# Attention output by query rows and a later transpose, in place of an output that is transposed from the start

## The chip, the cores and the metric

The kernel runs on one core of a Trainium2 chip. The metric is the device time of one execution in microseconds (us); lower is better. The engines are TensorE (PE, with its weight loads shown apart as PEld), VectorE (DVE), ScalarE (ACT), GpSimd (POOL) and SyncE (SP). All of them run their own instructions in order and wait for each other by semaphores. Matrix products are written to PSUM, which has eight banks per partition here.

## What is computed

Two parts follow each other: an attention over sorted blocks, and an expert layer on its output. Cut to what matters:

```python
# attention: B=4, H=8, S=768, D=64, 8 blocks of 96 rows
P = sort_net                                   # (4, 8, 8, 8)
for _ in range(5):                             # rows and columns made to sum to one
    P = exp(P - P.max(-1)); P /= P.sum(-1); P /= P.sum(-2)
k_s = einsum('bhij,bhjcd->bhicd', P, k_blocks); v_s = the same with v
attn = softmax(q_block @ k_s.T / 8)            # 96 x 96 per block
x = attn @ v_s                                 # -> (3072, 512): 4*768 rows, 8*64 columns
# expert layer: 3072 rows, 512 columns, 8 experts, 1024 hidden
G = exp(x @ w_gate - max)
for _ in range(8):                             # Sinkhorn rounds
    G /= G.sum(1); G /= G.sum(0); G *= 3072 / 8
out = sum over e of G[:, e] * (relu(x @ w1[e]) @ w2[e])
```

## The kernel before

**Stages.** (1) 0 to 14.4 us: the sorting matrix is made by DVE and ACT while PE runs 36 products that nobody reads (L131). `Pbig` is copied out of PSUM (L157). (2) The attention, from 14.4 us. (3) Sinkhorn on the gates `glog` (L348 to L360). (4) The gates go to DRAM and back (L370, L389), and the expert layer runs in 24 units (from L672 on), seven products of a Strassen scheme each. PE's first product of unit 0 starts at 154.1 us.

**The attention loop (L295 to L315).** Sixteen pairs of heads go through three steps, and 19 iterations `m` run them staggered: `stage1(m)`, `stage2(m-1)`, `stage3(m-2)`.

- `stage1` (L173) sorts K and V with products against the expanded matrix `R` (L182), transposes Q (L193), and copies five PSUM banks to SBUF: three by ACT (L187), V's second and Q by DVE (L189, L196). It then builds the next pair's `R` on DVE (L167).
- `stage2` (L200) makes the scores of eight blocks (L208), has ACT take their exponential into `ATT` (L211), transposes V (L215) and lets DVE copy it to `VS` (L218). There the 96 rows of a block lie on partitions, and each of 8 blocks x 2 heads has 64 columns.
- `stage3` (L220) works in two halves of four blocks. A product with `ones64` (L226) puts the sums of the exponentials on 64 partitions for each head. ACT makes the reciprocal out of Ln and Exp (L229, L230). The products of L234 have `VS` as weights and `ATT` as the moving side, so that the output has head columns on partitions, 64 for each head of the pair. DVE multiplies by the reciprocal and writes `xtT` (L236), which is x transposed.

Between the steps stands `fill(1)`, four per iteration. It gives PE a block of the expert layer's first product (`h_block`, L259: four products of 512 columns, L264), as soon as the batches that it reads are done (`state["done"]`, L315); before that, it gives a product that nobody reads (`spin`, L277, L280). The blocks' relu goes to DVE (L268) and ACT (L270) in turn; there are 88 blocks in all. `gate(b)` (L240) makes the gate logits of a batch (L244) and their exponential (L246). Up to iteration 5 the fills are spins.

All PSUM tiles here come from one pool of eight banks (`bank`). A bank is given out again when its last reader is done.

**Sinkhorn.** Each of eight rounds runs on DVE: row sums (L349), reciprocal (L350), product (L351), column sums (L353). Three blocks go to PE (`fill(3)`), then the matmul that adds over partitions (L356), and DVE ends the round (L357, L358). Then `gbf` is copied (L363), one block follows (`fill(1)`), `gp` is transposed (L367), copied to `gTs` (L369) and sent out. Eight differences of weights (`w2_sums(0, ...)`, L346, two for each of four results) stand next, and at last the remaining 11 blocks.

**What sets the order.** Each part is recorded under a manual schedule, in which an engine's instructions keep the order of the source. Two parts that follow each other (the Sinkhorn part and the expert part) are recorded apart.

Of the kernel before, what the change touches and what calls it, by code (L numbers as in the profile page):

```python
# [13 lines left out]
F32 = mybir.dt.float32  # L14
BF16 = mybir.dt.bfloat16
F16 = mybir.dt.float16
AF = mybir.ActivationFunctionType
AX = mybir.AxisListType
ALU = mybir.AluOpType
ENG = mybir.EngineType  # L20

def mkap(t, dims, off=0):
    return bass.AP(tensor=t.tensor, offset=t.offset + off, ap=dims)

@with_exitstack
def kernel(
# [11 lines left out]
    nc = tc.nc  # L38
    B, H, S, D = 4, 8, 768, 64
    NB = 8  # L40
    NPAIR = 16
    N, Dm, E, F = 3072, 512, 8, 1024
    NT = 24
    KB = 1024
    scale = 1.0 / (D ** 0.5)

    ones = ctx.enter_context(tc.tile_pool(name="ones", bufs=1))
# [3 lines left out]
    def bank(shape, dt=F32):  # L51
        return ps.tile(shape, dt, name="bank")
# [3 lines left out]
    def carve(shape, dt, off):  # L56
        n = 1
        for d_ in shape[1:]:
            n *= d_
        n = n * (2 if dt == F32 else 1)  # L60
        v_ = bigf[:, off // 2:off // 2 + n]
        if dt == F32:
            v_ = v_.bitcast(F32)
        names = "abcd"[:len(shape) - 1]
        return v_.rearrange("p (" + " ".join(names) + ") -> p " + " ".join(names),
                            **{k_: d_ for k_, d_ in zip(names, shape[1:])})
# [3 lines left out]

    warm = ones.tile([128, 1], F32)
    nc.vector.memset(warm, 0.0)
    nc.scalar.preload_act_table_set("natural_log_exp_and_others")
    nc.scalar.activation(out=warm, in_=warm, func=AF.Exp)

    wide = carve([128, 512], BF16, 98 * KB)
# [1 line left out]
    ident = ones.tile([128, 128], BF16)  # L78
    make_identity(nc, ident)
    identh = ones.tile([128, 128], F16)  # L80
    nc.vector.tensor_copy(identh, ident)
    ones64 = ones.tile([128, 64], BF16)
    nc.vector.memset(ones64, 1.0)
    ones32 = ones.tile([128, 128], F32)
    nc.vector.memset(ones32, 1.0)
    mask = ones.tile([128, 16], F32)
# [7 lines left out]
    atp_ = actx.enter_context(tc.tile_pool(name="atp", bufs=2))  # L94
# [13 lines left out]
    w1t, w2t = {}, {}  # L108

    def load_w1(e):  # L110
        w1t[e] = w1r[W1S[e]]
        nc.gpsimd.dma_start(out=w1t[e], in_=moe_w1[e].rearrange("(kk k) f -> k kk f", k=128))
# [10 lines left out]
    xtT = ones.tile([128, 4, B, 6, 128], BF16)  # L123
# [14 lines left out]
    for it in range(5):  # L138
# [4 lines left out]
                                op=ALU.mult)  # L143
        nc.vector.reduce_sum(out=rs, in_=Pt, axis=AX.X)
        nc.vector.reciprocal(out=rs, in_=rs)
        if it < 4:
            nc.vector.tensor_tensor(out=Pt, in0=Pt, in1=mkap(rs, [rs.ap[0], rs.ap[1], [0, 8]]),
                                    op=ALU.mult)
        else:
            nc.vector.tensor_tensor(out=Prep, in0=mkap(P, [P.ap[0], [8, 8], [1, 8], [0, 16]]),  # L150
                                    in1=mkap(rs, [rs.ap[0], [0, 8], [1, 8], [0, 16]]), op=ALU.mult)
# [4 lines left out]
    Pbig = carve([128, 8, 32], F32, 90 * KB)  # L156
    nc.vector.tensor_copy(Pbig, pbp)  # L157

    KT, VT, QT, ATT, VS = {}, {}, {}, {}, {}

    vs_ = [carve([128, 8, 2, 64], BF16, (91 + 3 * n) * KB)[0:96] for n in range(2)]

    Rt = {}

# [35 lines left out]
    def stage2(m):  # L200
        ATT[m] = [atp_.tile([96, 2, 384], BF16, name=f"at{h2}") for h2 in range(2)]
        for half in range(2):
            bb = [bank([96, 4, 96]) for _ in range(2)]
            for i4 in range(4):
                i = half * 4 + i4
                for h2 in range(2):
                    hs = slice(64 * h2, 64 * h2 + 64)
                    nc.tensor.matmul(bb[h2][:, i4, :], KT[m][hs, i].rearrange("d kk c -> d (kk c)"),  # L208
                                     QT[m][hs, :, 16 * i:16 * i + 16], start=True, stop=True)
            for h2 in range(2):  # L210
                nc.scalar.activation(out=ATT[m][h2][:, half, :], in_=bb[h2].rearrange("k i q -> k (i q)"),  # L211
                                     func=AF.Exp, scale=scale)
        b_ = bank([96, 8, 128], BF16)
        for i in range(8):
            nc.tensor.matmul(b_[:, i, :], VT[m][:, i].rearrange("d kk c -> d (kk c)"), ident, is_transpose=True,  # L215
                             start=True, stop=True)
        VS[m] = vs_[m % 2]
        nc.vector.tensor_copy(VS[m], b_.rearrange("c i (h d) -> c i h d", d=64))  # L218

    def stage3(m):  # L220
        b, hpi = m // 4, m % 4
        xo = xtT[:, hpi, b].rearrange("d kk (i c) -> d i kk c", c=16)
        for half in range(2):
            den = bank([128, 384])
            for h2 in range(2):
                nc.tensor.matmul(den[64 * h2:64 * h2 + 64, :], ones64[0:96], ATT[m][h2][:, half, :],  # L226
                                 start=True, stop=True)
            rc = atp_.tile([128, 384], F32, name="rc")
            nc.scalar.activation(out=rc, in_=den, func=AF.Ln)  # L229
            nc.scalar.activation(out=rc, in_=rc, func=AF.Exp, scale=-1.0)  # L230
            b_ = bank([128, 4, 96])
            for i4 in range(4):
                for h2 in range(2):
                    nc.tensor.matmul(b_[64 * h2:64 * h2 + 64, i4, :], VS[m][:, half * 4 + i4, h2, :],  # L234
                                     ATT[m][h2][:, half, 96 * i4:96 * i4 + 96], start=True, stop=True)
            nc.vector.tensor_tensor(out=xo[:, 4 * half:4 * half + 4],  # L236
                                    in0=b_.rearrange("d i (kk c) -> d i kk c", c=16),
                                    in1=rc.rearrange("d (i kk c) -> d i kk c", i=4, c=16), op=ALU.mult)

    def gate(b):  # L240
        b_ = bank([128, 6, E])
        for t in range(6):
            for kk in range(4):
                nc.tensor.matmul(b_[:, t, :], xtT[:, kk, b, t, :], wg[:, kk], start=(kk == 0),  # L244
                                 stop=(kk == 3))
        nc.scalar.activation(out=glog[:, 6 * b:6 * b + 6, :], in_=b_, func=AF.Exp)  # L246
# [35 lines left out]
    def fill(n, both=True):  # L282
        for _ in range(n):
            if state["h"] >= len(blocks):
                return
            e, c, fb = blocks[state["h"]]
            if last_batch[c] > state["done"]:
                if state["done"] < 0:
                    spin(1)
                return  # L290
            h_block(e, c, fb, both)
            state["h"] += 1

    build_r(0)
    for m in range(NPAIR + 3):  # L295
        if m < NPAIR:
            stage1(m)
        if m + 4 < NPAIR:
            load_pair(m + 4)
        if m == 0:  # L300
            load_w1(0)
        if m == 5:
            load_w1(1)
        fill(1)
        if 1 <= m <= NPAIR:
            stage2(m - 1)
        fill(1)
        if 2 <= m <= NPAIR + 1:
            stage3(m - 2)
        fill(1)  # L310
        if m >= 6 and m % 4 == 2:
            gate(m // 4 - 1)
        fill(1)
        if m >= 5 and m % 4 == 1:
            state["done"] = m // 4 - 1  # L315

    order.__exit__(None, None, None)
# [5 lines left out]
    w2T = [r2.tile([128, 2, 4, 256], BF16, name=f"w2T{n}") for n in range(3)]  # L323
# [14 lines left out]
    rs2 = ones.tile([128, NT], F32)  # L338
    cs2 = ones.tile([128, E], F32)
    cs1 = ones.tile([128, E], F32)  # L340
    def w2_sums(p, k, i):
        w = w2t[2 * p + i]
        B11, B12, B21, B22 = (w[:, 4 * fh:4 * fh + 4, 256 * dh:256 * dh + 256] for fh in range(2) for dh in range(2))
        T1, T2, T4 = (t[:, i] for t in w2T)
        o_, a, b = ((T1, B12, B11), (B12, B22, B12), (T2, B22, T1), (T4, B21, T2))[k]
        nc.vector.tensor_tensor(out=o_, in0=a, in1=b, op=ALU.subtract)  # L346

    for it in range(8):  # L348
        nc.vector.reduce_sum(out=rs2, in_=glog, axis=AX.X)  # L349
        nc.vector.reciprocal(out=rs2, in_=rs2)  # L350
# [1 line left out]
                                op=ALU.mult)  # L352
        nc.vector.reduce_sum(out=cs2, in_=glog.rearrange("p t e -> p e t"), axis=AX.X)  # L353
        fill(3, both=False)
        b_ = bank([128, E])
# [3 lines left out]
                                       in1=mkap(cs1, [cs1.ap[0], [0, NT], cs1.ap[1]]),  # L359
# [1 line left out]
    gbf = ones.tile([128, E, NT], F16)  # L361
    gTs = carve([128, 2, 128], BF16, 108 * KB)[0:96].bitcast(F16)
    nc.vector.tensor_copy(gbf, glog.rearrange("p t e -> p e t"))  # L363
    fill(1, both=False)
    gp = bank([96, 2, 128], F16)
    for n in range(2):
        nc.tensor.matmul(gp[:, n, :], gbf.rearrange("p e t -> p (e t)")[:, 96 * n:96 * n + 96], identh,  # L367
                         is_transpose=True, start=True, stop=True)
    nc.vector.tensor_copy(gTs, gp)  # L369
    nc.sync.dma_start(out=gdr.rearrange("(n r) p -> r n p", n=2), in_=gTs)  # L370
    for k in range(4):
        for i in range(2):
            w2_sums(0, k, i)
    fill(len(blocks), both=False)
    order.__exit__(None, None, None)
    pctx.close()
# [23 lines left out]
    def w1_sums(e, part):  # L400
        w = w1t[e]
        A11, A12, A21, A22 = (w[:, 2 * kh:2 * kh + 2, 512 * fh:512 * fh + 512] for fh in range(2) for kh in range(2))
        S1, S2, S4 = wS[e % 2]
        o_, a, b, op = ((S1, A21, A22, ALU.add), (S2, S1, A11, ALU.subtract), (A21, A11, A21, ALU.subtract),
                        (S4, A12, S2, ALU.subtract))[part]
        nc.vector.tensor_tensor(out=o_, in0=a, in1=b, op=op)

    def relu_add(out, a, b):
        nc.vector._custom_dve(TENSOR_ADD_SAT, out=out, in0=a, in1=b, s0=3.4028234663852886e38, s1=0.0)  # L409
# [194 lines left out]
    for n in range(3, NU):  # L604
        nq = NDQ.get(n, 4)
        nd = min(nq, len(l1) - first_dq)
        for d_ in range(nd):
            for st in range(4):
                q = 28 * n + (28 * d_) // nq + (0, 3, 5, 9)[st] * (28 // nq) // 7
# [3 lines left out]
    for q in sorted(when):  # L613
        for d_, st in when[q]:
            if st == 3:
                k_, e, c, j = l1[d_]
# [2 lines left out]
    load_gates(0)  # L619
    load_gates(1)  # L620
    load_w1(2)
    for fh in range(2):
        for i in range(2):
            gate(0, i, 4 * fh, 4 * fh + 4)
# [88 lines left out]
```

## Time and profile before

| what | value |
|---|---|
| median of 3 runs | 686.58 us (686.45 to 687.9) |
| the profiled execution | 687.9 us |
| its span, from the first to the last instruction | 685.8 us |
| PE busy | 670.4 us (98%) |
| DVE busy | 536.0 us (78%) |
| ACT busy | 338.5 us (49%) |
| POOL busy | 121.6 us (18%) |
| granted TensorE clock, mean | 0.998 |

Rows of a timeline have the start and the duration in us, the engine, the line, the operation, the tiles written and read (out<-in), their shapes and the number of instructions that were merged into the row. In brackets stands how long the engine was idle before it, and what ended that. Two instructions of one engine can overlap by some 0.1 us, so what an instruction costs its engine is the distance from its start to the next one's. Ends of matrix products are modelled: their starts are what counts.

### The profile page before, as it was taken

Reading aid. Unit: us, or ns where it says so; the run is one execution under the profiler, and the core shown is the slowest. Engines: PE = TensorE matmul, PEld = TensorE weight load, DVE = VectorE, ACT = ScalarE, POOL = GpSimd, SP = SyncE. Lnnn points to the kernel's source line nnn. Section 1 sums busy time; section 2 is a strip of 40 time slices with the busy share of each in tenths; the row PEclk is TensorE's granted clock in tenths of the full one; section 3 lists DMA queues with packets and bytes.
Section 4 is the critical chain, followed back from the end, with each engine's and each line's share of the span. In section 5 each row is a group of like instructions: output and inputs, shape, how many; then the busy total and the mean of one; then the engine's idle time right before and its main releaser. Section 6 shows DMA issues by size and latency. Waiting matters only on the chain.

```text
span 685.8 us, 15431 instructions
## 1 busy us (share of the span) xinstructions
PE 670.4 (98%) x6524; PEld 547.1 (80%) x6550; DVE 536.0 (78%) x748; ACT 338.5 (49%) x646; POOL 121.6 (18%) x163
## 2 busy tenths in 40 slices
PE   7999999999998999999999999999999999999997
PEld 3665655448787888888888888888888888888886
DVE  6666565789789888887887897787688897687776
ACT  2888887663322444444544444444444444444441
POOL 8543000000212111221122032022022022102201
PEclk9999999999999999999999999999999999999999
DMA  9996208032362919540455668353176044145335
GB/s 143 205 204 96 36 3 124 0 73 66 114 153 72 194 60 196 96 74 9 74 78 84 118 95 135 50 78 44 34 116 99 4 77 77 17 63 78 37 88 123
DMA packets 45940, 59.77 MB, mean 87 GB/s; under 512 B 3760, under 2 KB 31408, under 8 KB 45744
## 3 DMA queue, kind: packets, MB, share of 16 engines
q0 software_dynamic: 37840, 50.35, 46.3%
q1 hardware_dynamic: 7616, 8.05, 4.1%
q8 instruction: 51, 0.84, 0.5%
q10 hardware_dynamic: 416, 0.39, 0.2%
q14 instruction: 17, 0.14, 0.1%
HBM read 59.79 MB, written 25.21 MB: 124 GB/s over the span
## 4 chain that ended last, share of the span: by engine, by line
PE 87%; DVE 9%; ACT 2%; issue 2%; DMA 0%; ACTq 0%; DVEq 0%
PE bank L264 11%; DVE bigf L471 2%; PE bank L182 2%; DVE bigf L409 1%; PE bank L215 1%; PE bank L208 1%; PE a_8682 L509 1%; PE a_6377 L509 1%; PE a_7824 L509 1%; PE a_4052 L509 1%; PE a_3122 L509 1%; PE a_2988 L509 1%; PE a_7536 L509 1%; PE a_4347 L509 1%; PE a_3304 L509 1%
## 5 line engine op out<-in xcount | busy, mean ns | idle before, releaser
L509 PEld LDWEIGHTS <-bigf 128*128 128x128 bf16 x1520 | 148.7, 98 | 18.3
L518 POOL DMA_DIRECT2D out_dram<-bigf x92 | 72.3, 901 | 428.7 <-DVE bigf L528 404.9
L431 PEld LDWEIGHTS <-bigf 128*128 128x128 bf16 x1248 | 122.1, 98 | 18.8 <-issue 4.6
L471 DVE TENSOR_TENSOR bigf<-bigf 128x2048 bf16<-128x2048 bf16 (+1 forms) x68 | 111.1, 1657 | 0.2 <-DMA bigf<-gdr 0.2
L270 ACT ACTIVATE bigf<-bank 128x512 bf16<-128x512 f32 x62 | 37.0, 597 | 17.9 <-PE bank L264 17.5
L264 PE MATMUL bank<-xtT,w1r_88 128*128 128x512 bf16 x178 | 45.2, 379 | 0.7
L236 DVE TENSOR_TENSOR xtT<-bank,rc 128x384 bf16<-128x384 f32 x32 | 17.9, 558 | 31.2 <-ACT rc L230 30.1
L509 PEld LDWEIGHTS <-hS_2661 128*128 128x128 bf16 x384 | 37.5, 98 | 5.7 <-issue 1.0
L431 PEld LDWEIGHTS <-w1r_89 128*128 128x128 bf16 x384 | 37.5, 98 | 5.3 <-issue 1.0
L431 PEld LDWEIGHTS <-w1r_88 128*128 128x128 bf16 x384 | 37.6, 98 | 5.0 <-issue 0.7
L509 PEld LDWEIGHTS <-hS_2660 128*128 128x128 bf16 x384 | 37.6, 98 | 4.8
L509 PEld LDWEIGHTS <-hS_2662 128*128 128x128 bf16 x384 | 37.6, 98 | 4.6
L264 PE MATMUL bank<-xtT,w1r_89 128*128 128x512 bf16 x152 | 37.5, 380 | 0.5
L485 DVE TENSOR_TENSOR hS_2660<-bigf 128x2048 bf16<-128x2048 bf16 x24 | 29.3, 1219 | 2.5 <-PE g_3202 L509 2.2
L264 PEld LDWEIGHTS <-w1r_88 128*128 128x128 bf16 x192 | 17.3, 100 | 17.0
L485 DVE TENSOR_TENSOR hS_2661<-hS_2660,bigf 128x2048 bf16<-128x2048 bf16 x24 | 29.3, 1221 | 0.2
L485 DVE TENSOR_TENSOR bigf<-bigf 128x2048 bf16<-128x2048 bf16 x24 | 29.3, 1219 | 0.1
L485 DVE TENSOR_TENSOR hS_2662<-bigf,hS_2661 128x2048 bf16<-128x2048 bf16 x24 | 29.2, 1219 | 0.0
L264 PEld LDWEIGHTS <-w1r_89 128*128 128x128 bf16 x160 | 14.6, 99 | 15.4
L268 DVE TENSOR_SCALAR bigf<-bank 128x512 bf16<-128x512 f32 x26 | 17.5, 684 | 1.2 <-PE bank L264 1.2
L230 ACT ACTIVATE rc<-rc 128x384 f32<-128x384 f32 x32 | 16.7, 522 | 1.0
L187 ACT CAST KT<-bank 128x384 bf16<-128x384 f32 x32 | 13.7, 481 | 6.9 <-PE bank L182 6.7
(1404 smaller groups left out, 1504.7 us busy)
## 6 DMA issues: line engine op xcount, KB each, us to landing
out_dram<-bigf POOLq DMA_DIRECT2D x92, 256.0 KB, 5.5
bigf<-gdr SPq DMA_DIRECT2D x24, 256.0 KB, 7.4
bigf<-in_moe_w_dram POOLq DMA_DIRECT2D x6, 1024.0 KB, 13.9
kb<-in_k_dram POOLq DMA_DIRECT2D x16, 192.0 KB, 7.0
vb<-in_v_dram POOLq DMA_DIRECT2D x16, 192.0 KB, 7.0
qb<-in_q_dram POOLq DMA_DIRECT2D x16, 192.0 KB, 7.2
w1r_88<-in_moe_w_dram POOLq DMA_DIRECT2D x3, 1024.0 KB, 10.4
w1r_89<-in_moe_w_dram POOLq DMA_DIRECT2D x3, 1024.0 KB, 11.5
```

The source lines that it names most:

```text
L182: nc.tensor.matmul(b_[64 * h2:64 * h2 + 64, k3, :], src[:, h2, 3 * kh2 + k3, :], R[:, h2].rearrange("p i c -> p (i c)"), start=True, stop= ...
L187: nc.scalar.copy(dst, b_)
L230: nc.scalar.activation(out=rc, in_=rc, func=AF.Exp, scale=-1.0)
L236: nc.vector.tensor_tensor(out=xo[:, 4 * half:4 * half + 4], in0=b_.rearrange("d i (kk c) -> d i kk c", c=16), in1=rc.rearrange("d (i kk c) ...
L264: nc.tensor.matmul(b_, w1t[e][:, kk, fb * 128:(fb + 1) * 128], xf[:, kk, c * 512:(c + 1) * 512], start=(kk == 0), stop=(kk == 3))
L268: nc.vector.tensor_scalar_max(hT[e, c][:, fb, :], b_, 0.0)
L270: nc.scalar.activation(out=hT[e, c][:, fb, :], in_=b_, func=AF.Relu)
L431: nc.tensor.matmul(b_[:, i, :], A[:, kk, 128 * (2 * j + i):128 * (2 * j + i) + 128], Bm[:, kk, :], start=(first and i == 0 and kk == 0), s ...
L471: nc.vector.tensor_tensor(out=h, in0=h, in1=mkap(g, [g.ap[0], [0, f1 - f0], [1, 512]]), op=ALU.mult)
L485: nc.vector.tensor_tensor(out=o_, in0=a, in1=b, op=op)
L509: nc.tensor.matmul(b_[:, g, :], A[P_][i][:, j, 128 * g:128 * g + 128], Bm[P_][i][:, j, :], start=(first and i == 0 and g == 0 and j == 0), ...
L518: nc.gpsimd.dma_start(out=out[bb * S:(bb + 1) * S].rearrange("(p kk) d -> kk p d", kk=6)[kk], in_=o_[:, tt, :], accum_op=ALU.add if p else ...
```

## The change

Its short description reads: "Last unit adds the other passes' sums on chip and stores by hardware DMA in quadrants; first pass copies one PSUM bank by ScalarE; longer warm-up spin, in place of: Attention output comes out already" (it breaks off there). The diff does the following.

- `VS` gets a 65th column of ones for each block and head, set once by two memsets on DVE behind the copy of `Pbig`. `ones64` goes.
- `stage3` now has `ATT` as weights (96x96) and 65 columns of `VS` as the moving side: 16 products per pair, in four banks, with query rows on partitions and the sum of the exponentials as column 65. For each bank DVE takes the reciprocal of four sums and multiplies by it into a new tile `OG`. The 4 products of `ones64`, the 16 products of 96 columns, the 4 Ln/Exp activations and the 2 products of 384 columns on DVE go.
- A new `stage4` transposes `OG` by 8 products with the identity into one bank, and ACT copies it to `xtT`. It runs one iteration later, so the loop has 20 iterations, and `gate` and `state["done"]` move back by one: iterations 0 to 6 are filled with spins.
- The `fill(1)` between `gbf` and the transposes of `gp` goes; the last fill has 12 blocks in place of 11.
- `w2_sums(0, ...)` is called in the next part, behind `load_w1(2)` and ahead of the first `gate`. In the program that results, its eight instructions stand on DVE's queue inside the first Sinkhorn rounds (they depend on nothing in them); the order of all else on DVE from Sinkhorn on is that of before.
- The preloading of ACT's table is left to the first activation.

Line numbers of the changed kernel that are used below: 188, 195, 166 and 217 are the old 189, 196, 167 and 218; 226, 229, 230 are stage3's products, reciprocal and product; 237 and 239 are stage4's transposes and copy; Sinkhorn's 346, 347, 348, 350, 354, 355 are the old 349, 350, 351, 353, 357, 358; 406 is `w2_sums`.

```diff
-    ones64 = ones.tile([128, 64], BF16)
-    nc.vector.memset(ones64, 1.0)
...
-    vs_ = [carve([128, 8, 2, 64], BF16, (91 + 3 * n) * KB)[0:96] for n in range(2)]
+    vs_ = [carve([128, 8, 2, 65], BF16, (91 + 3 * n) * KB)[0:96] for n in range(2)]
+    for t in vs_:
+        nc.vector.memset(t[:, :, :, 64:65], 1.0)
...
-        nc.vector.tensor_copy(VS[m], b_.rearrange("c i (h d) -> c i h d", d=64))
+        nc.vector.tensor_copy(VS[m][:, :, :, 0:64], b_.rearrange("c i (h d) -> c i h d", d=64))
 
     def stage3(m):
+        OG[m] = atp_.tile([96, 8, 2, 64], BF16, name="OG")
+        for half in range(2):
+            for h2 in range(2):
+                b_ = bank([96, 4, 65])
+                for i4 in range(4):
+                    i = half * 4 + i4
+                    nc.tensor.matmul(b_[:, i4, :], ATT[m][h2][:, half, 96 * i4:96 * i4 + 96],
+                                     VS[m][:, i, h2, :], start=True, stop=True)
+                rc = atp_.tile([96, 4], F32, name="rc")
+                nc.vector.reciprocal(out=rc, in_=b_[:, :, 64:65].rearrange("q i a -> q (i a)"))
+                nc.vector.tensor_tensor(out=OG[m][:, 4 * half:4 * half + 4, h2, :], in0=b_[:, :, 0:64],
+                                        in1=mkap(rc, [rc.ap[0], [1, 4], [0, 64]]), op=ALU.mult)
+
+    def stage4(m):
         b, hpi = m // 4, m % 4
...
+        b_ = bank([128, 8, 96], BF16)
+        for i in range(8):
+            nc.tensor.matmul(b_[:, i, :], OG[m][:, i].rearrange("q h d -> q (h d)"), ident[0:96, 0:96],
+                             is_transpose=True, start=True, stop=True)
+        nc.scalar.copy(xtT[:, hpi, b].rearrange("d kk (i c) -> d i kk c", c=16),
+                       b_.rearrange("d i (kk c) -> d i kk c", c=16))
...
-    for m in range(NPAIR + 3):
+    for m in range(NPAIR + 4):
...
         if 2 <= m <= NPAIR + 1:
             stage3(m - 2)
         fill(1)
+        if m >= 7 and m % 4 == 3:
+            gate(m // 4 - 1)
+        if 3 <= m <= NPAIR + 2:
+            stage4(m - 3)
+        fill(1)
         if m >= 6 and m % 4 == 2:
-            gate(m // 4 - 1)
-        fill(1)
-        if m >= 5 and m % 4 == 1:
             state["done"] = m // 4 - 1
...
     nc.vector.tensor_copy(gbf, glog.rearrange("p t e -> p e t"))
-    fill(1, both=False)
     gp = bank([96, 2, 128], F16)
...
     nc.sync.dma_start(out=gdr.rearrange("(n r) p -> r n p", n=2), in_=gTs)
-    for k in range(4):
-        for i in range(2):
-            w2_sums(0, k, i)
     fill(len(blocks), both=False)
...
     load_w1(2)
+    for k in range(4):
+        for i in range(2):
+            w2_sums(0, k, i)
     for fh in range(2):
```

## The prediction

> **What bounds the kernel now.** First the chain of work that ended last: it is TensorE (PE) for most of the span, and its VectorE (DVE) pieces lie at 203 to 220 us and later, outside what is changed.
>
> ```profile
> PE 87%; DVE 9%; ACT 2%; issue 2%; DMA 0%; ACTq 0%; DVEq 0%
> ```
>
> Then the busy time by stretch. The columns after the stretch are its length and the busy us of PE, weight loads, DVE, ACT (ScalarE) and POOL.
>
> ```profile
> 14.40:38.80 24.40, 23.89 (x439) 16.55 (x439) 14.45 (x29) 20.78 (x52) 14.57 (x21) 0.93 1.30 203
> 38.80:105.40 66.60, 65.73 (x1009) 39.92 (x1024) 42.05 (x78) 56.88 (x132) 12.56 (x17) 1.00 0.51 76
> 105.40:143.00 37.60, 37.34 (x255) 18.36 (x254) 24.38 (x60) 25.10 (x47) 0.00 (x0) 1.00 0.32 52
> 143.00:154.10 11.10, 10.87 (x53) 4.97 (x53) 10.01 (x16) 7.17 (x13) 0.75 (x1) 1.00 0.55 109
> ```
>
> The stretches are iterations 0 to 5 (filled with spins), iterations from 6 on (filled with blocks), the tail with Sinkhorn, and the last blocks before unit 0. PE is full in all of them. But a full PE can be full of waiting, so the first stretch is read on ACT's timeline. It stands in the window of iterations 2 to 5:
>
> ```profile
> 29.14 0.52 ACT L229 ACTIVATE rc<-bank 128x384 f32<-128x384 f32 x1
> 29.70 0.52 ACT L230 ACTIVATE rc<-rc 128x384 f32<-128x384 f32 x1
> 30.12 0.47 ACT L229 ACTIVATE rc<-bank 128x384 f32<-128x384 f32 x1
> 30.63 0.52 ACT L230 ACTIVATE rc<-rc 128x384 f32<-128x384 f32 x1
> 31.06 0.84 ACT L187 CAST KT<-bank 128x384 bf16<-128x384 f32 x2
> 31.79 0.49 ACT L187 CAST VT<-bank 128x384 bf16<-128x384 f32 x1
> 32.16 0.50 ACT L211 ACTIVATE at_699<-bank 96x384 bf16<-96x384 f32 x1
> ```
>
> No idle bracket stands on any row: ACT runs without a gap from one L229 (29.14) to that of the next iteration (33.66), 4.5 us, of which Ln and Exp take 31.06-29.14 = 1.92. So iterations 2 to 5 are bound by ACT, which the change relieves. From 38.84 on an iteration takes 6.64 us (86.73 to 93.37) and the products stand end to end; there PE bounds.
>
> **PE: the attention output.** Rows of one iteration:
>
> ```profile
> 88.83 0.43 PEld L208 LDWEIGHTS <-KT 64*96 64x96 bf16 x16 [0.42 <-issue]
> 89.31 0.50 PEld L215 LDWEIGHTS <-VT 128*96 128x96 bf16 x8
> ```
> ```profile
> 90.76 0.35 PE L226 MATMUL bank<-at_1910,ones_76 96*64 96x384 bf16 x1
> ...
> 91.55 1.90 PE L264 MATMUL bank<-xtT,w1r_88 128*128 128x512 bf16 x8
> ```
>
> Old: 91.55-90.76 = 0.79, plus the 0.09 between the end of the last block product (89.80 + 4 x 0.216 = 90.66) and the first load: 0.88 us per pair. The 0.09 recurs where the shape of the array changes (to L208, to L226, back); the new products use the whole array like the blocks, and lose it. New stage3: 16 products with 96-column weights and 65 moving columns. Two such loads with their 96-column products start every (0.43-0.12)/7 = 44 ns in L208, one with 128 columns every (0.50-0.12)/7 = 54 ns in L215. By moving columns alone the price would be 65/96 of the 42 ns of L234 (0.36 us, in four pairs), 28 ns; if load and product didn't overlap, 44+28 = 72. I take 44, the row with the same load: 16 x 0.044 = 0.70. Stage4: 8 transposes with 96 moving columns, 42 ns each as in L234 (54 at most, L215): 0.34. So 1.04 for 0.88.
>
> [...]
>
> **DVE in the early iterations.** From start to start, its rows take: L189 0.47, L196 0.46, L167 0.34, L218 0.61. New are four reciprocals (0.21 by L357, which reads 128x8 from PSUM; 0.19 to 0.30 by L145 and L350) and four products of 256 columns (0.42: L167 has 256 columns, and L236 with 384 takes 0.558). Start to start a pair takes 0.235+0.34 = 0.575, four take 2.30; DVE needs 4.18 per iteration. PE needs the 3.16 of iteration 1 (18.13 to 21.29, four spins, no attention output) plus 0.70 plus 0.34 = 4.20. ACT needs 4.5-1.92+0.83 = 3.4, with the stage4 copy at 0.83 (L187 0.48 for 384 columns, L270 0.60 for 512, carried on to 768; 0.5 to 1.0 would be hidden too). So ACT's 4.5 becomes 4.2, set by PE and DVE at once: little is gained, and the new lead is thin.
>
> **L218 with rows of 65.** It copies 1024 bf16 in 0.69 us, L196 768 in 0.55: 0.53 ns per column, half of L189's f32 rate. Its output rows now start 130 bytes apart. If that loses the pairing, it costs 0.55 + 640 x 1.03 ns = 1.21 (L189, carried on with the slope from L189 to L268). I take 0.69, since the operation and types stay.
>
> [...]
>
> **Sum up to Sinkhorn.** Two memsets now stand between L157 and the first L167, for which PE waits (0.98): 2 x 0.07 (L72 0.06, L83 0.11), +0.15. Spins now fill iterations 0 to 6. Old iterations 2 to 5 took 38.84-21.29 = 17.55. New 2 takes 3.16+0.70 = 3.86 and 3 to 6 take 4 x 4.2 = 16.8: +3.1 at the first block. By then one stage1 (1.23) and one stage2 (1.07) more are done: -2.30. Of the rest, old had 12 x 0.88 = 10.56; new has 11 x 0.70 + 12 x 0.34 = 11.78: +1.2. DVE needs 4.18 + 2 x 0.60 (L268) = 5.4 of 6.8 there, so it stays hidden. Subtotal +2.15.
>
> **New waits.** A reciprocal waits for its stage3 bank; behind it on DVE stand the next iteration's VT and QT copies. PE's QT product now waits for a bank that DVE's last product frees: in block iterations that comes 2.5 us after stage3 ends (two blocks, stage4, half of stage1) and DVE needs 2.3; in spin iterations this is why DVE's 4.18 counts in full. Stage4 waits for products of the iteration before, long done. The first block of a batch waits for the 0.83 copy of stage4, with a spin and a stage1 (1.4 us) in between.
>
> **The eight weight sums.** In the changed kernel's instruction order they no longer follow gTs. DVE gets them early in Sinkhorn (new line numbers): one between L348 and L350 of round 1, one behind its L355, one each behind L346, L347, L348 and L350 of round 2, one between L354 and L355, one behind L355.
>
> ```profile
> 142.41 0.50 DVE L353 TENSOR_REDUCE cs_2673<-glog 128x8 f32<-128x192 f32 x1
> 143.46 0.21 DVE L357 RECIPROCAL cs_2674<-bank 128x8 f32<-128x8 f32 x1 [0.54 <-PE bank L356]
> ...
> 144.09 0.33 DVE L363 CAST gbf<-glog 128x192 f16<-128x192 f32 x1
> ...
> 145.10 0.69 DVE L346 TENSOR_TENSOR w2T_2657<-w2r_2655 128x1024 bf16<-128x1024 bf16 x1
> 145.71 0.69 DVE L346 TENSOR_TENSOR w2T_2657<-w2r_2656 128x1024 bf16<-128x1024 bf16 x1
> ```
>
> Today they lie in the wait for the gates' transfer (free at 150.0, gates at 150.17), at no cost. In Sinkhorn a round takes 2.79, PE's three blocks and its matmul (3 x 0.86 + 0.21) all of it, and DVE ends L353 at 142.91 for a matmul at 143.07: the slack is 0.1. A sum between two dependent operations costs its 0.605 (start to start) less the 0.11 that they lie apart anyway, 0.5. Round 1 has slack (L353 ends at 122.16, the matmul starts at 123.57): the first is free. Ahead of round 2's matmul stand four: 2.0-0.1 = 1.9. Ahead of round 3's stand three, one of them in the 0.54 wait (0.1), two at 0.5: 1.1-0.1 = 1.0. Together +2.9: PE, in order, has only three blocks ahead of each matmul. Bounds: 0 and 8 x 0.605 = 4.84. The w2 loads land at 116.9, long before.
>
> **The block that moved.** Old PE computed one block (0.86) while DVE finished gbf (143.28 to 144.14); now it idles and does the block after the transposes: +0.86 (0 if unit 0 waited for the gates; but its products start right behind the last block, and the gates then come earlier than needed).
>
> **Behind unit 0** order and work are the same. PE waits 0.8 us at 203 and 2.3 at 220 for DVE, but DVE waited for PE at 189.24, so a delay passes through. Sum: 2.15+2.9+0.86 = **+5.9 us**. The profiled execution took 687.9 with a span of 685.8, 1.3 above the median 686.58; its span would be 691.7, and on the median I predict **692.5 us**.
>
> **Rivals.**
> - L218 at 1.21: DVE needs 4.70 in iterations 3 to 6, 4 x 0.5 = +2.0 and some in iteration 2: 694.7. For: the odd pitch. Against: same types. 24%.
> - The sums find cover (PE has a queue of blocks): -2.9, 689.6. Against: the column-sum matmul stands in PE's order behind three blocks only. 8%.
> - Not slower: ScalarE's relief shortens the iterations with blocks too. ACT is busy 56.88 of 66.60 there; if PE's fullness hid waits for it, 12 iterations times 0.5 would give -6.0: 686.5. It decides from -0.38 per iteration on (5.9-1.4 over 12), that is, if PE's own work is at most 6.26 of 6.64. Against: its products are spaced at full rate (4 x 0.216 per block). 4%.
> - Loads don't overlap (72 ns): 16 x 0.45 = +7.2, 699.7. 4%.
> - The change does what its short description says (hardware stores in the last unit, a longer warm-up) and not what the diff says: nothing in the diff touches the last unit's stores or the 36 warm-up products of L131, so nothing is gained there. Under 1%.
>
> **Numbers.** The forecast has 60%: 691 to 694 with reciprocals at 0.19 to 0.30. The range takes in the first rival with the same spread, and leaves out the other three (16%): 690.0 to 695.8. About 0.2%, 1.4 us, is what a measurement here can tell from no change. All but the third rival are slower by more: slower 96%, same 3%, faster 1%.
>
> **What would show it.** Right: ACT with gaps in iterations 3 to 6, at about 4.2 us; the new L226 products about 44 ns apart; L217 at 0.69; three Sinkhorn rounds of which the second takes about 4.7 and the third 3.8; PE idle about 1.2 before the gp transposes; unit 0 starting at about 160 (154.1). Wrong: an L217 of 1.2, rounds of 2.8 throughout, or a block iteration under 6.6.

## The result, and the profile after

The changed kernel takes 694.43 us, the median of 4 runs (692.39 to 695.53), against 686.52 us beside it (686.39 to 687.9): a ratio of 1.0107, with a 95% interval of 1.0079 to 1.0135. It is slower. Its profiled execution took 693.87 us with a span of 691.7, which is the span that the prediction gives; the median is 1.9 above the predicted 692.5. One of the four runs, 695.53 us, has a span of only 691.8: 3.7 us of it lie outside the span, where the other three have 2.0 to 2.2. What they are is not known.

The chain that ended last is PE as before:

```profile
PE 87%; DVE 8%; DMA 2%; issue 2%; ACT 1%; POOL 0%; ACTq 0%; POOLq 0%; DVEq 0%
```

Busy time of the changed kernel by stretch, columns as in the prediction (length; PE, weight loads, DVE, ACT, POOL; then granted clock, DMA share, GB/s). The stretches are iterations 3 to 6, those with blocks, Sinkhorn's second and third round, the later rounds, and the last blocks up to unit 0:

```profile
23.79:40.95 17.16, 17.16 (x354) 13.72 (x353) 16.18 (x50) 13.69 (x32) 10.22 (x15) 1.00 1.29 203
40.95:103.50 62.55, 61.60 (x954) 41.43 (x972) 48.97 (x130) 42.55 (x93) 10.87 (x15) 1.00 0.53 82
124.41:132.68 8.27, 5.81 (x29) 2.56 (x28) 7.66 (x19) 4.18 (x7) 0.00 (x0) 1.00 0.00 0
132.68:147.90 15.22, 14.15 (x71) 6.83 (x72) 11.29 (x33) 8.96 (x15) 0.00 (x0) 1.00 0.01 2
147.90:158.45 10.55, 10.46 (x50) 4.86 (x51) 5.36 (x6) 6.57 (x11) 0.75 (x1) 1.00 0.68 128
```

In iterations 3 to 6 PE is full and DVE nearly so (17.16 and 16.18 of 17.16), and ACT no longer is: an iteration takes 17.16 / 4 = 4.29, where the prediction has 4.2 and the old kernel 4.5. The third line is the one that is new in kind: PE works for 5.81 of 8.27 us, while DVE is busy for 7.66.

ACT's timeline of the changed kernel in iterations 3 and 4 has the gaps that the old one lacked (the bracket is the idle time before a row):

```profile
27.98 0.80 ACT L239 COPY xtT<-bank 128x768 bf16<-128x768 bf16 x1 [0.64 <-PE bank L237]
28.67 0.87 ACT L186 CAST KT<-bank 128x384 bf16<-128x384 f32 x2
...
32.41 0.80 ACT L239 COPY xtT<-bank 128x768 bf16<-128x768 bf16 x1 [0.73 <-PE bank L237]
```

DVE in the same window, with the small reciprocal, the product, and the copy into rows of 65:

```profile
28.82 0.17 DVE L229 RECIPROCAL rc<-bank 96x4 f32<-96x4 f32 x1
29.02 0.42 DVE L230 TENSOR_TENSOR OG<-bank,rc 96x256 bf16<-96x256 f32 x1
...
30.93 0.69 DVE L217 COPY bigf<-bank 96x1024 bf16<-96x1024 bf16 x1 [0.22 <-PE bank L214]
```

The copy takes 0.69, as L218 did with rows of 64: the odd row pitch costs nothing here, and the first rival falls. Stage3 on PE, in an iteration with blocks:

```profile
93.71 0.33 PE L226 MATMUL bank<-bigf,at_2147 96*96 96x65 bf16 x4
93.88 0.35 PE L226 MATMUL bank<-bigf,at_2148 96*96 96x65 bf16 x4
...
94.24 0.35 PE L226 MATMUL bank<-bigf,at_2148 96*96 96x65 bf16 x4
94.42 0.81 PE L266 MATMUL bank<-xtT,w1r_85 128*128 128x512 bf16 x3
```

From start to start the 16 products take 94.42-93.71 = 0.71, 44 ns each, as the prediction took them; an iteration with blocks takes 6.81.

DVE in the second Sinkhorn round, and the last step ahead of PE's matmul in the third:

```profile
125.25 0.68 DVE L406 TENSOR_TENSOR w2T_2840<-w2r_2839 128x1024 bf16<-128x1024 bf16 x1
125.86 0.34 DVE L346 TENSOR_REDUCE rs_2855<-glog 128x24 f32<-128x192 f32 x1
126.12 0.68 DVE L406 TENSOR_TENSOR w2r_2838<-w2r_2838 128x1024 bf16<-128x1024 bf16 x1
126.72 0.29 DVE L347 RECIPROCAL rs_2855<-rs_2855 128x24 f32<-128x24 f32 x1
126.93 0.63 DVE L406 TENSOR_TENSOR w2r_2839<-w2r_2839 128x1024 bf16<-128x1024 bf16 x1
127.47 0.34 DVE L348 TENSOR_TENSOR glog<-glog,rs_2855 128x192 f32<-128x192 f32 x1
127.74 0.68 DVE L406 TENSOR_TENSOR w2T_2841<-w2r_2838,w2T_2840 128x1024 bf16<-128x1024 bf16 x1
128.34 0.49 DVE L350 TENSOR_REDUCE cs_2856<-glog 128x8 f32<-128x192 f32 x1
...
132.03 0.50 DVE L350 TENSOR_REDUCE cs_2856<-glog 128x8 f32<-128x192 f32 x1
```

And PE, which waits for the column sums of L350 and then for `gbf`:

```profile
124.41 0.28 PE L353 MATMUL bank<-cs_2856,ones_75 128*128 128x8 f32 x2
...
128.97 0.36 PE L353 MATMUL bank<-cs_2856,ones_75 128*128 128x8 f32 x2 [1.67 <-DVE cs_2856 L350]
...
132.68 0.36 PE L353 MATMUL bank<-cs_2856,ones_75 128*128 128x8 f32 x2 [0.74 <-ACT bigf L272]
```
```profile
147.94 0.31 PE L363 MATMUL bank<-identh,gbf 128*96 128x128 f16 x2 [1.06 <-DVE gbf L360]
```

Four sums stand ahead of the second round's L350 and each puts it back: the matmuls stand 4.56 and 3.71 us apart where later ones stand 2.8 apart. In the third round the bracket names ACT, whose relu had to free the bank; but L350 ends at 132.53 (132.03 + 0.50) on DVE and the relu at 132.57 (131.97 + 0.60) on ACT, so both ended together.

**The granted clock.** One thing is not seen in either kernel's order of instructions. Windows of the changed kernel around PE's 2.3 us wait at 222.11:

```profile
222.04:225.45 3.41, 1.10 (x10) 0.87 (x9) 2.68 (x4) 1.67 (x4) 2.61 (x5) 1.00 0.41 150
225.45:228.85 3.40, 3.40 (x18) 2.43 (x16) 3.40 (x4) 0.98 (x2) 1.33 (x2) 0.50 0.98 208
228.85:232.26 3.41, 3.41 (x34) 3.05 (x32) 2.44 (x2) 0.83 (x2) 0.00 (x0) 1.00 1.16 171
```

For 3.4 us PE gets half the clock (18 products where the next stretch has 34). The run of the changed kernel that has the highest mean clock has a span 1.5 us shorter (690.2 against 691.7). The profiled execution of the kernel before has no such stretch there, though it waits as long; it has one at its start:

```profile
14.50:17.95 3.45, 3.12 (x39) 2.21 (x39) 1.45 (x3) 1.24 (x3) 2.30 (x4) 0.51 1.48 193
```

That one costs 1.3 us: iteration 0 took 3.70 there and 2.40 in the changed kernel. In the 45 later runs of the kernel before, on three chips, the span takes three values: 684.4 to 684.6 in 17 (mean clock 0.999 or 1.000), 685.6 to 685.9 in 19 (0.996 to 0.998), 687.1 to 687.5 in 9 (0.995). The changed kernel's four spans are 690.2 (0.999), 691.7, 691.8 (0.998) and 693.0 (0.995). The profiled executions with a mean clock of 0.996 to 0.998 have one such stretch, and those with 0.995 (in e1, e5, e8 and e9 below) have two. So, by its clock, a run of these two kernels draws none, one or two, and runs without any differ by 690.2-684.4 = 5.8.

### The profile page after: what moved, and what is told of

It reads as the page before. It is cut to its first block, busy times and chain, and to the rows that moved or that the text cites. A ratio compares the mean times of both kernels' runs of the same rounds, so it can differ in the third digit from the quotient of the medians.

```text
span 691.7 us, 15580 instructions
## 1 busy us (share of the span) xinstructions
PE 674.5 (98%) x6590; PEld 556.1 (80%) x6618; DVE 552.1 (80%) x845; ACT 322.7 (47%) x598; POOL 121.5 (18%) x163
## 4 chain that ended last, share of the span: by engine, by line
PE 87%; DVE 8%; DMA 2%; issue 2%; ACT 1%; POOL 0%; ACTq 0%; POOLq 0%; DVEq 0%
PE bank L266 10%; DMA qb<-in_q_dram 2%; DVE bigf L471 2%; PE bank L181 2%; PE bank L226 2%; DVE bigf L409 1%; PE bank L214 1%; PE bank L207 1%; PE a_5110 L509 1%; PE a_8865 L509 1%; PE a_4018 L509 1%; PE a_3305 L509 1%; PE a_7719 L509 1%; PE a_6846 L509 1%; PE a_6560 L509 1%
## 5 line engine op out<-in xcount | busy, mean ns | idle before, releaser
L230 DVE TENSOR_TENSOR OG<-bank,rc 96x256 bf16<-96x256 f32 x64 | 26.9, 420 | 2.2
L266 PEld LDWEIGHTS <-w1r_86 128*128 128x128 bf16 x160 | 14.6, 99 | 14.5
L239 ACT COPY xtT<-bank 128x768 bf16<-128x768 bf16 x16 | 12.8, 798 | 14.1 <-PE bank L237 13.6
```

The lines of the kernel that those rows point to most:

```text
L230: nc.vector.tensor_tensor(out=OG[m][:, 4 * half:4 * half + 4, h2, :], in0=b_[:, :, 0:64], in1=mkap(rc, [rc.ap[0], [1, 4], [0, 64]]), op=AL ...
L266: nc.tensor.matmul(b_, w1t[e][:, kk, fb * 128:(fb + 1) * 128], xf[:, kk, c * 512:(c + 1) * 512], start=(kk == 0), stop=(kk == 3))
```

## The experiments

Clean below means a run with a mean clock of 0.999 or 1.000. Lines of the experiments are up to 7 higher or lower than the changed kernel's.

**The eight sums back behind gTs** (e1_sums_back), on the changed kernel:

```diff
     nc.sync.dma_start(out=gdr.rearrange("(n r) p -> r n p", n=2), in_=gTs)
+    for k in range(4):
+        for i in range(2):
+            w2_sums(0, k, i)
     fill(len(blocks), both=False)
...
     load_w1(2)
-    for k in range(4):
-        for i in range(2):
-            w2_sums(0, k, i)
```

> The changed kernel with its eight weight sums put back behind the copy of gTs; nothing else. Theory of the prediction: the sums cost what rounds 2 and 3 of Sinkhorn grew by. In the trace of the changed kernel the column-sum matmuls of these rounds stand 4.56 and 3.71 us behind the ones before, where later rounds take 2.80: (4.56-2.80)+(3.71-2.80) = 2.7. So about -2.7 us, the fastest run at about 689.7 where that of the changed kernel is 692.39, and all rounds at 2.8. Rival (cover): PE's later blocks would have taken the time anyway; then 0, and 692.4. Second question, the spread of the changed kernel's runs (692.39 to 695.53, mean clocks 0.999 to 0.995): if PE's idle stretches of 1.67 and 0.74 us in Sinkhorn bring the half-clock stretches, the runs lie within 1.7 us of the fastest with clocks of 0.998 or more; if they come from elsewhere (the 2.3 us wait behind unit 1 stands in both kernels), the spread stays at about 3 us.

692.38 us (689.76 to 692.76, 6 runs; ratio to before 1.0062, 1.0044 to 1.0079). The clean run has a span of 687.6, 2.6 below the changed kernel's 690.2, and the rounds stand 2.73 and 2.80 apart: the sums cost what was said. But four of six runs have the clock of two half-clock stretches (0.995), with PE busy for 15.5 of 15.6 us from 124.4 on in the profiled one: these do not come from idle time in Sinkhorn.

**Also one block back ahead of gp** (e3_both_back):

```diff
+    fill(1, both=False)
     gp = bank([96, 2, 128], F16)
```

> The changed kernel with the eight sums back behind gTs and one block back between gbf and the transposes of gp: only the attention's new form is left of the change. Theory: the block costs what PE's idle time there shows, 0.87 more than the sums alone, so -3.6 from the changed kernel (fastest run about 688.8), and +2.1 (the prediction's subtotal 2.15) over the kernel before (fastest 686.39, so 688.5). Rival (cover): the block is work that PE has to do sometime, and unit 0 waits for the gates; then no gain over the sums alone. Rival (attention form costs nothing by itself): 686.4. The runs' spread: as for the sums alone, and smaller still if PE's 1.06 us of idle time ahead of gp counts.

690.35 us (689.66 to 692.02, 6 runs; ratio 1.0046, 1.0032 to 1.006). Clean span 686.6: 1.0 less than with the sums alone (0.87 expected), and 2.2 over the clean 684.4 of the kernel before, which is the attention's new form alone (subtotal 2.15). The time of that one run does not show the 1.0: it is 689.66, only 0.1 below the clean run of e1 and above the 688.8 expected, because 3.1 us of it lie outside the span, where e1's has 2.2. The runs with one stretch (0.998) do show it, with spans of 687.9 to 688.2 against 689.0.

**Only the sums moved, in the kernel before** (e4_before_sums; the edit of e1 the other way round):

> The kernel before, with only its eight weight sums moved to where the changed kernel calls them. Theory: +2.7 (prediction 2.9), from two longer Sinkhorn rounds: fastest run 689.1 against 686.4. Rival (interaction): the sums cost time only together with the new attention output, then 686.4. The spread: if PE's idle time in Sinkhorn brings half-clock stretches, some of these runs are 1.3 to 3.4 us above the fastest with clocks of 0.997 or less; if not, they spread as those of the kernel before (686.39 to 687.9).

691.48 us (689.29 to 695.03, 8 runs; ratio 1.0061, 1.0041 to 1.0081). Clean spans 687.1 and 687.2: +2.75, without any change to the attention. The sums got other places in DVE's order here; one round takes it all:

```profile
126.31 0.35 PE L349 MATMUL bank<-cs,ones 128*128 128x8 f32 x2
126.52 2.75 PE L264 MATMUL bank<-xtT,w1r 128*128 128x512 bf16 x12
131.94 0.36 PE L349 MATMUL bank<-cs,ones 128*128 128x8 f32 x2 [2.67 <-DVE cs L346]
```

The spread is wider than that of the kernel before: one run has a span of 693.0 at a clock of 0.990, 5.9 above the clean ones, which is more than two stretches. It was not profiled. The profiled run (0.996) has one stretch, at 14.5 us, and none behind the wait of 2.67 us.

**Sinkhorn's idle time filled** (e5_spins), on the changed kernel: `spin(6)` and `spin(2)` ahead of the column-sum matmuls of rounds 2 and 3, `spin(4)` ahead of `gp`.

> The changed kernel with products that nobody reads put into PE's three idle stretches of Sinkhorn: six (1.3 us) ahead of round 2's column-sum matmul (idle 1.67), two (0.43) ahead of round 3's (0.74), four (0.86) ahead of the transposes of gp (1.06). They end before DVE lets the matmuls go, so the path is the same: fastest run 692.4. If PE's idleness in Sinkhorn brings the half-clock stretches, the runs come together at 692.4 to 693; if not, they spread to 695 as those of the changed kernel do. If the products delay the path after all, the fastest run is later than 692.6.

695.08 us (693.51 to 695.32, 5 runs; ratio 1.0105, 1.0089 to 1.012). The rounds are 4.56 and 3.71 apart as before, so the path is the same, and none of the five runs is clean; the profiled one has its two stretches at 14.2 and 225.8 us. So the half clock of the changed kernel does not need Sinkhorn's idle time. That the longer wait in e4 never brings it is not shown.

**PE's two long idle stretches closed**, in the changed kernel (e6_after_noidle) and in the kernel before (e7_before_noidle):

```diff
-    for _ in range(36):
+    for _ in range(41):
...
+    w_ = bank([128, 512])
+    for _ in range(4):
+        nc.tensor.matmul(w_, wide[:, 0:128], wide, start=True, stop=True)
     Pbig = carve([128, 8, 32], F32, 90 * KB)
...
-            at(ks[k], h_sum, n, k)
+            if (n, k) in ((4, 3),):
+                at(ks[k], h_sum, n, k, 0, 1)
+                at(ks[k], h_sum, n, k, 1, 2)
+            else:
+                at(ks[k], h_sum, n, k)
```

> The changed kernel with PE's two long idle stretches closed, nothing of the change undone. (a) 41 products in place of 36 ahead of the sorting matrix, and 4 more that nobody reads while PE waits for the copy of Pbig. (b) The 2.3 us for which PE waits at 222 us: ScalarE's copy there waits for the last sum of unit 4's h (L485), whose one instruction reads two tiles through a stride that spans the copy's buffer; that sum is cut into two instructions, one for each tile. Theory on the spread: the half-clock stretch of 3.41 us follows such an idle stretch (at 14.5 us, and at 225.45 behind the wait at 222.1), so here all runs lie within 0.5 us of each other with a clock of 0.999 or 1.000, at 692.3-2.3 = 690.0. Rival: the stretches come at random or from Sinkhorn's idle time; then the spread stays at 3 us. Rival for (b): the wait only moves on, to DVE; then the fastest run stays at 692.

> The kernel before with the same two idle stretches closed in the same way. Theory: all runs together at 686.5-2.3 = 684.2. With the kernel above it gives what the change costs when no half clock is in either: by the prediction's steps +5.9, by the two traces' positions (unit 0 +5.6, 0.3 given back at 203) +5.4. Rival: if half-clock stretches are part of what the change itself does to the time, the two kernels' medians still differ by the 7.9 of the medians 694.43 and 686.52.

e6: 690.81 us (690.67 to 691.06, 6 runs; ratio 1.0041, 1.0026 to 1.0055). e7: 685.05 us (685.05 to 685.18, 5 runs; ratio 0.9957, 0.9941 to 0.9973). The spread falls to 0.4 and 0.1 us (one of e6's six runs has a clock of 0.998, the others 0.999 or 1.000), and neither profiled execution has a stretch at 14.5 or 225 us. So the two idle stretches brought the half clock; they were closed together, not one by one. What the change costs without them is 690.81-685.05 = **5.8 us** (prediction 5.9). The long wait is gone; what is left of e6's waits of PE from 118 to 240 us is this (engine, tile, line, what it waited for: us in total, times, longest):

```profile
PE bank L356 <- DVE cs L353: 1.7, 1, 1.7
PE bank L366 <- DVE gbf L363: 1.1, 1, 1.1
PE bank L356 <- ACT bigf L275: 0.7, 1, 0.7
PE a L512 <- ACT cps L535: 0.5, 1, 0.5
PE a L434 <- DVE bigf L412: 0.2, 1, 0.2
```

In the kernel before, closing the wait gives 684.4-682.9 = 1.5 us of span, not the 2.3 expected; what takes back the rest was not followed.

**ACT relieved by a reciprocal on DVE** (e8_half_recip), and with the idle stretches closed (e9_best), on the kernel before. Both runs also have one spin per iteration in place of four from iteration 2 on, and the eight banks in fixed turn; the lines below show the reciprocal only:

```diff
-            nc.scalar.activation(out=rc, in_=den, func=AF.Ln)
-            nc.scalar.activation(out=rc, in_=rc, func=AF.Exp, scale=-1.0)
+            if m < 4 and half == 0:
+                nc.vector.reciprocal(out=rc, in_=den)
+            else:
+                nc.scalar.activation(out=rc, in_=den, func=AF.Ln)
+                nc.scalar.activation(out=rc, in_=rc, func=AF.Exp, scale=-1.0)
```

> The kernel before, form of the attention unchanged, but ACT relieved otherwise: for the first four pairs the reciprocal of the first half is made by DVE in place of ACT's Ln and Exp; one spin per iteration in place of four from iteration 2 on; the eight PSUM banks in fixed turn. It asks whether iterations 2 to 5 (4.5 us each) were bound by ACT, as the prediction says. Theory: ACT needs 4.5-0.96 = 3.54 and DVE 3.0+0.47 = 3.5, PE 3.16+0.88-0.65 = 3.4, so 3.55 an iteration and about -3.6 in all: fastest run 682.9. Rival: the loads of K, V and Q (pair 5 lands at 29.3 us) or PE bound them as well; then 4.0 or more an iteration, and -2 at most. Rival: the fixed turn of banks adds waits and eats the gain (686).

> The relief of ACT above and the two closed idle stretches together, on the kernel before. Theory: the gains add, 686.5-3.6-2.3 = 680.6, all runs within 0.5 us of each other. Rival: DVE, which is full from 203 to 225 us, takes back what unit 0 starts earlier; then about 682 to 683.

e8: 693.52 us (690.61 to 693.94, 6 runs; ratio 1.0073, 1.0054 to 1.0093). e9: 689.85 us (688.72 to 691.08, 10 runs; ratio 1.003, 1.0016 to 1.0044). Both expectations fall, and the price that was furthest off is the reciprocal's. DVE and PE of e8 in iteration 3:

```profile
23.15 2.54 DVE L233 RECIPROCAL rc<-bank 128x384 f32<-128x384 f32 x1
...
25.75 0.53 PE L196 MATMUL bank<-ident,qb 128*64 128x128 bf16 x12 [1.76 <-DVE rc L233]
```

A reciprocal of 384 columns takes 2.54 us, not 0.47: 6.6 ns per column, where a copy of as many takes 0.55 (L192). PE waits 1.76 for a bank behind it and gets half clock afterwards (a granted clock of 0.50 from 27.66 to 31.07). What the fixed turn of banks costs by itself was not separated. So these runs say nothing on ACT; the runs below ask again.

**What bounds the early iterations.** Both kernels with closed idle stretches, without spins from iteration 2 (e10_before_nospin) or 3 on (e12_after_nospin), and then with copies moved off the engine in question: two from ACT to DVE (e11_before_nospin_copies), one from DVE to ACT (e13_after_nospin_copy).

```diff
-                if state["done"] < 0:
+                if state["done"] < 0 and m < 2:
...
-                if nm == "KT" or kh2 == 0:
+                if (nm == "KT" or kh2 == 0) and not ((nm == "VT" or kh2 == 1) and 2 <= m <= 5):
```

(For the changed kernel `m < 3`, and `or 3 <= m <= 6` at the end of the old second condition.)

> The kernel before with the two idle stretches closed (685.05), and without the four spins per iteration from iteration 2 on (0.86 us of PE each). It asks what bounds iterations 2 to 5. Theory (ACT, 4.5 us without a gap): PE only gets gaps, iterations 3 to 5 stay at 4.5, and the time within 0.5 us of 685.05 (iteration 2, where ACT is not yet full, may give up to 0.9). Rival (PE is the bound): iterations of 3.65, and 685.05-3.4 = 681.6.

684.82 us (684.49 to 684.86, 4 runs; ratio 0.9947, 0.9926 to 0.9968). Iterations 4 and 5 take 4.51 each, as with spins. (Iterations 2 and 3, with 3.16 and 4.11, are 1.3 shorter together than in e7, and iteration 6, with 8.43, is 1.0 longer: PE runs ahead and then waits for ACT.) Iterations 4 and 5 stand in this window, whose PE is free for 1.5 us of 9.02 while ACT is not:

```profile
27.21:36.23 9.02, 7.51 (x168) 6.02 (x164) 5.95 (x13) 8.89 (x24) 6.66 (x10) 1.00 1.31 201
```

> The same, and two of ACT's three copies of stage1 (0.42 each from start to start) made by DVE in iterations 2 to 5. Theory: ACT falls to 3.66, DVE rises to 3.0+0.9 = 3.9, so iterations of 3.9 to 4.2 and about -1.3 to -2 against the run without spins. Rival (loads, or waits for banks): 4.5 as before.

683.2 us (683.07 to 683.61, 4 runs; ratio 0.9925, 0.9904 to 0.9946). Iterations 3 to 5 take 4.30 on average (4.78, 3.77 and 4.34), more than the 3.9 to 4.2 expected and little less than e10's 4.38. But iteration 6 takes 7.29 in place of 8.43: iterations 2 to 6 take 23.35 us together, against 24.72 in e10 and 24.98 in e7. The run is 1.6 faster than e10, the fastest kernel here, 3.3 below a run of the kernel before without half clock (686.5).

> The changed kernel with the two idle stretches closed (690.81), and without the spins from iteration 3 on (four per iteration, 0.86 us of PE). The prediction has PE at 4.20 and DVE at 4.18 as equal bounds of iterations 3 to 6. Theory: DVE holds, iterations stay at 4.2, time within 0.5 us of 690.8. Rival (DVE has slack, only PE binds): 3.35 each, and 690.8-3.4 = 687.4.

691.04 us (690.97 to 692.71, 8 runs; ratio 1.0047, 1.0033 to 1.006). Iterations 3 to 6 take 16.88, 4.22 on average, as DVE's 4.18 has it. PE is free for 1.1 of 8.76 in the last two of them (DVE's 7.82 leaves out the short pauses between its rows, which follow each other but for 0.7 us of waiting in the last three iterations):

```profile
31.92:40.68 8.76, 7.67 (x171) 6.75 (x169) 7.82 (x25) 7.14 (x16) 6.35 (x9) 1.00 1.30 204
```

In these two iterations, of 4.37 and 4.39, DVE is not all of it: PE waits there for banks that ACT's copy of stage4 (L242) has to free, 0.26 and 0.43 us, and DVE's 0.7 of waiting is for PE's products of L217.

> The same, and V's second copy (0.47) made by ACT in place of DVE in iterations 3 to 6. Theory: DVE 4.18-0.47 = 3.71, ACT 3.4+0.42 = 3.8, PE 3.35, so iterations of 3.8 and about -1.6 against the run without spins (689.2). Rival (a wait across the engines, not DVE's work, is the bound): 4.2 again.

690.97 us (690.82 to 691.33, 9 runs; ratio 1.0044, 1.0029 to 1.0059). Iterations 3 to 6 fall to 3.95 on average (3.8 expected; a wait across the engines alone would have left them at 4.2), Sinkhorn's first matmul comes 0.66 earlier, and unit 0 starts 0.2 later all the same: its first product now waits 0.69 for ACT's last relu (L275). Why that wait is there was not tried.

## Why the prediction was right

Positions in e6 and then in e7, where no half clock is in either: iteration 0, the first iteration with blocks, the first column-sum matmul, the transposes of `gp`, and unit 0.

```profile
14.45 0.53 PE L184 MATMUL bank<-R,kb 128*64 128x128 bf16 x12
41.09 0.53 PE L184 MATMUL bank<-R,kb 128*64 128x128 bf16 x12
124.56 0.28 PE L356 MATMUL bank<-cs,ones 128*128 128x8 f32 x2
148.09 0.31 PE L366 MATMUL bank<-identh,gbf 128*96 128x128 f16 x2 [1.06 <-DVE gbf L363]
158.59 1.91 PE L512 MATMUL a<-w2r,bigf 128*128 128x256 bf16 x16
```
```profile
14.37 0.53 PE L185 MATMUL bank<-R,kb 128*64 128x128 bf16 x12
37.49 0.53 PE L185 MATMUL bank<-R,kb 128*64 128x128 bf16 x12
122.21 0.28 PE L359 MATMUL bank<-cs,ones 128*128 128x8 f32 x2
143.13 0.31 PE L370 MATMUL bank<-identh,gbf 128*96 128x128 f16 x2 [0.18 <-DVE gbf L366]
152.78 1.91 PE L512 MATMUL a<-w2r,bigf 128*128 128x256 bf16 x16
```

The change's steps in the prediction's order (us):

| step | predicted | measured | how |
|---|---|---|---|
| memsets | 0.15 | 0.08 | iteration 0 starts at 14.45, not 14.37; not shown, since it starts at 14.37 in e12 too, which has the memsets |
| iterations up to the first block | 3.1 | 3.5 | 41.09 against 37.49, less 0.08 |
| attention after that | -1.1 | -1.25 | first column-sum matmul 124.56 against 122.21 |
| eight sums | 2.9 | 2.6 | 23.53 against 20.92 from there to gp |
| block behind gp | 0.86 | 0.85 | from gp to unit 0: 10.50 against 9.65 |
| behind unit 0 | 0 | 0 | unit 0 +5.81, span +5.8 |
| sum | 5.9 | 5.8 | |

The sum is nearer than its terms: 0.4 too little for the first iterations is made up by 0.3 too much for the sums and 0.15 and 0.07 elsewhere. Unit 0 and the end are late by the same 5.8, so nothing is gained in the last unit, and the rival that took the short description at its word falls.

- *Which engine bound the early iterations, and what is late next.* Right. For the old form it is shown: without spins iterations 4 and 5 stay at 4.51 with ACT busy for 8.89 of 9.02, and with two copies taken off ACT they fall to 3.77 and 4.34. For the new form DVE's work is shown to be a part of it (4.22, and 3.95 with one copy less on DVE); waits between PE and ACT have a share that was not separated. Mis-sized by 0.4: iterations 3 and 4 of the changed kernel took 4.30 and 4.43, not 4.2.
- *The prices on PE and DVE.* Right: 44 ns per product, 0.69 for the copy, 0.55 per pair of reciprocal and product (0.575 said). The rivals on the copy, on loads that don't overlap (72 ns) and on shorter iterations with blocks (6.81, not under 6.6) fall with these rows. The 0.09 at the change of shape does not come in the new form, as said: four block products start from 92.85 on, and the first new product at 92.85 + 4 x 0.216 = 93.71. What the prediction calls the pairing was seen only as a price, 0.53 ns per bf16 column (L196, L218) against 1.03 per f32 column (L189, L268). That rows 130 bytes apart might lose it was the author's guess, and 1.21 an estimate at the f32 price; the 0.69 of L217 shows nothing lost.
- *The sums in Sinkhorn.* Right in mechanism and nearly in size, not covered by PE's queue of blocks (e1: -2.6), and independent of the attention's form (e4: +2.75). In e4, with another order of the sums, the cost is the same: what counts is that DVE's chain is the round.
- *The half clock* is the step that failed, though the range was wide enough for it. "1.3 above the median" was taken as a mark of one execution; it was the 1.3 us of half clock in its iteration 0, and the 0.93 in the first of the prediction's window lines said so. The forecast of 692.5 holds for a run without such a stretch (692.39), and three of four runs of the changed kernel had one or two by their clocks (0.998, 0.998, 0.995). That is also why unit 0 starts at 158.45 and not at 160, though the span agrees to 0.1 us: the profiled execution of before had its stretch ahead of unit 0, that of after behind it. That each of the two had just one is luck.

## What to carry to other kernels

Instructions that depend on nothing still cost time when they stand inside a chain of short dependent steps on an engine that runs in order: here 2.6 to 2.75 of the 4.84 us that the eight take, while the same eight were free in a wait for a transfer (in the kernel before, the last ends at 150.01 and the gates are there for DVE at 150.17). Taking work off the bound engine gains only up to the next limit: here an iteration went from 4.5 to 4.3 us, and the extra iteration of the longer pipeline cost more than that gained (2.2 us for the attention as a whole). Before two medians are compared, look at each run's clock: in the changed kernel a wait of PE of 2.3 us was followed by 3.4 us at a granted clock of 0.50, and with the two long idle stretches closed the times repeat within 0.4 us.

## What the runs showed of the hardware

In two profiled executions the half-clock stretches lie on a grid whose step is their length, 3.41 us. In e1 two start at about 15.6 and 223.8 us, 208.2 apart, 61 times 3.413; in e8 two start 10.24 apart, three times as much. In three executions, whether the wait of 2.3 us brought one went with where it fell on the grid: with PE busy for 1.10 of the 3.41 us ahead of a grid point, the next 3.41 us ran at a clock of 0.50 (222.04 above; in e1 1.10 from 220.44 on, and 0.50 from 223.85 on). In e4, whose grid goes by its stretch at 14.5 us (60 steps to 219.3), the same wait fell across a grid point and left 1.48, and the clock stayed at 1.00:

```profile
219.30:222.70 3.40, 1.48 (x14) 1.17 (x12) 2.96 (x5) 0.26 (x1) 1.21 (x3) 1.00 0.04 14
222.70:226.10 3.40, 3.02 (x28) 2.65 (x28) 3.04 (x3) 2.39 (x5) 2.73 (x4) 1.00 0.91 296
```

Busy time alone is not the measure, though: ahead of e8's stretch PE was busy for 1.78 of 3.41 (24.25 to 27.66), 0.67 of it with L211's products of 64 rows. What is counted stays open.

DVE's reciprocal took 6.6 ns per column in e8 (2.54 for 384, where a copy of as many took 0.55), and rows of the kernel before have much the same: 0.21 for 8 columns (L357) and 0.30 for 24 (L350), 0.09 for 16 more, 5.6 ns per column. At these prices the new form, with 4 columns (0.17), can use it, while for 384 columns Ln and Exp on ACT are cheaper (1.92 us for two such pairs).
